# One-lane steps: V's rows and layer B's transposes in another order, layer B on one lane's columns in three more passes, its last pass without mask products

## The chip, the cores and the metric

The kernel runs on one core of one Trainium2 chip. The metric is the device time of one execution in microseconds (us).

## What is computed

Two kinds of layers follow each other four times, A, B, A, B, over 2048 positions of width 640, each with a layernorm ahead of it and a residual sum behind it. A is attention by segments of 32 positions with 32 heads of 192 and 8 memory rows that one segment hands to the next, so its segments must be computed in order. B is attention with 32 heads of 20 over 8 positions of the past, two apart.

```python
# A, for each of the 64 segments s
h = concat([mem, xs])                               # 8 + 32 rows
q, k, v = h @ Wq, h @ Wk, h @ Wv                    # 32 heads of 192
o = softmax(mask(q k^T / sqrt(192))) v @ Wo
mem = o[:8]; outs.append(o[8:])
# B
idx = pos[:, None] - 2 * arange(8)[None, :]         # those below 0 are masked
o = softmax(q . k[idx] / sqrt(20)) v[idx] @ wo
# the whole
x = x + A(layernorm(x)); x = x + B(layernorm(x))
x = x + A(layernorm(x)); x = x + B(layernorm(x))
```

## The kernel before

**Steps and lanes.** The outer loop has 67 steps, t = 0 to 66. Both A layers share their weights, so a step computes one segment of the first A layer (lane 0, segment t) and one of the second (lane 1, segment t - 2) with the same weight loads; a lane has 40 columns (8 memory, 32 new), both have 80. Steps 0 and 1 have lane 0 alone, steps 64 and 65 lane 1 alone (`set_lanes`, `one_lane`). Layer B works one step behind, on `b = t - 1`, also with two lanes of 32 columns: lane 0 is the first B layer, lane 1 the second. Before, B computes all 64 columns in every step from 1 to 65, also in its passes of steps 1, 2 and 65, where only one lane has a segment. The last pass, step 66, is `b_alone`: one lane, nothing of A beside it.

**A step.** Its loop goes over 8 quads of 4 heads: key projection (`a_k`, L264, PSUM bank 0), query projection (bank 1), value projection (bank 2) with transposes in the next quad (`a_vt`), scores, exponential, mask, value product (`a_pv`), normalisation, and the output projection five quads later (`a_o`, L381). In one-lane steps, `a_v_rows` (L298, L299) computes V's rows directly for all quads but 2 and 3: the weights are the moving operand, in two halves of five matmuls of 384 columns, each copied by DVE into `Vt`. The first half uses bank 0 (bank 3 in quad 1), the second bank 2.

**Layer B inside a step.** Its pieces are spread by hand over the quads (`b_first`, `b_second` and `step`): layernorm statistics into bank 3 at quad 0, their centring and scaling by DVE at quad 1 (`ln_center` L456 writes into that bank, `ln_scale` L462 reads it and writes `h2T`), Q and K projections (`b_proj` L495, banks 0 and 3) at quad 1, V at quad 2, the queries spread over heads by POOL (`b_qexp` L526), the scores of four groups of 8 heads (`b_s` L538, banks 0 and 3) with the exponential on ACT and the mask product on DVE (`b_mask` L548), V's transposes (`b_vt` L516, copied by DVE, L520) at quad 3, value products (`b_pv` L561) and norms at quads 5 and 6, transposes of the result at quad 6 (`b_ot` L583) and the output projection (`b_wo` L594). In `b_alone` the same pieces follow each other, with `b_vt`'s two copies on ACT.

**Order.** The kernel writes out the order of PE, ACT, DVE, POOL and SP by hand: each engine takes its instructions in the order of the calls. Of the 64 halves of A's weights 41 stay on the chip; the other 23 are loaded again in each step into a ring of 4 buffers of 480 KB, by two loads of 240 KB each on SP's queue (L226). A ring load is issued when an earlier half's last matmul is done. The input of a step and the output of two segments go over ACT's queue (L606, L609).

Of the kernel before, what the change touches and what calls it, by code (L numbers as in the profile page):

```python
# [10 lines left out]
BF16 = mybir.dt.bfloat16  # L11
F32 = mybir.dt.float32
ACT = mybir.ActivationFunctionType
ALU = mybir.AluOpType
# [3 lines left out]
P = 128  # L18
D = 640
NC = 5  # L20
DH = 192
# [3 lines left out]
SEG = 32  # L25
LT = NM + SEG
NT = 2 * LT
NX = 2 * SEG
LAG = 2
# [4 lines left out]
BD = 20  # L34
BG = 8
# [43 lines left out]
class Kernel:  # L79
# [210 lines left out]
    def a_v_rows(self, i, t):  # L290

        nc = self.nc
        w = [self.units["v", i, h] for h in range(2)]
        vt = self.Vt[0:NT, :].rearrange("p (a b c) -> p a b c", a=2, b=2)
        for h in (1, 0):
            ps = self.big("ps_vr", (3 if i == 1 else 0) if h else 2)
            for c in range(NC):
                nc.tensor.matmul(ps[:, 0:2 * DH], lhsT=self.hT[:, NT * c:NT * c + P], rhs=w[h][:, c, :], start=(c == 0), stop=(c == NC - 1))  # L298
            nc.vector.tensor_copy(out=vt[:, h, :, 0:DH], in_=ps[0:NT, 0:2 * DH].rearrange("p (b c) -> p b c", b=2))  # L299
        self.used("v", i)  # L300

    def a_v(self, i, t):
# [187 lines left out]
    def b_proj(self, part, name, bank):  # L490
        nc = self.nc
        ps = self.big(name, bank)
        for n in range(NC):
            for c in range(NC):
                nc.tensor.matmul(ps[:, NX * n:NX * (n + 1)], lhsT=self.wqkv[:, part, c, P * n:P * (n + 1)], rhs=self.h2T[:, c, :],  # L495
                                 start=(c == 0), stop=(c == NC - 1))
        return ps[:, 0:NC * NX].rearrange("p (n x) -> p n x", n=NC)

    def b_k(self, b):
        self.nc.scalar.copy(out=self.KB[:, :, 64 * (b % 2):64 * (b % 2) + NX], in_=self.b_proj(1, "ps_bk", 3))  # L500

    def b_q(self, b):
        ps = self.b_proj(0, "ps_bq", 0)
        qb = self.bp.tile([P, 6, NX], BF16, name="QB")
        self.nc.scalar.copy(out=qb[:, 0:NC], in_=ps)  # L505
        self.qb = qb

    def b_v(self, b):

        self.nc.scalar.copy(out=self.VTB[:, :, 64 * (b % 2):64 * (b % 2) + NX], in_=self.b_proj(2, "ps_bv", 3))  # L510

    def b_vt(self, copy=None):
        nc = self.nc
        ps = self.ps_big.tile([P, NC, P], BF16, name="ps_bvt", tag="bank3")
        for n in range(NC):
            nc.tensor.transpose(out=ps[:, n, :], in_=self.VTB[:, n, :], identity=self.ident[:])  # L516
        W = BD + 1
        src = ps[:].rearrange("p n e -> p (n e)").rearrange("p (a h d) -> p a h d", a=2, d=BD)
        for par in range(2):
            (copy or nc.vector.tensor_copy)(out=self.VB[:, :, W * par:W * par + BD], in_=src[:, par])  # L520

    def b_qexp(self, c):
        h0, h1 = B_HEADS[c]
        nh = h1 - h0
        qx = self.ap2.tile([P, BG, NX], BF16, name="QX")
        self.nc.gpsimd.tensor_tensor(out=qx[:, 0:nh, :], in0=self.qb[:, c, :].unsqueeze(1).to_broadcast([P, nh, NX]),  # L526
                          in1=self.hmask[c][:].unsqueeze(2).to_broadcast([P, nh, NX]), op=ALU.mult)
        self.qxs[c] = qx

    def b_s(self, g):  # L530

        nc = self.nc
        ps = self.big("ps_bs", 3 * (g % 2))
        parts = [(c, max(h0, BG * g), min(h1, BG * (g + 1))) for c, (h0, h1) in enumerate(B_HEADS)]
        parts = [p for p in parts if p[1] < p[2]]
        for k, (c, lo, hi) in enumerate(parts):
            h0 = B_HEADS[c][0]
            nc.tensor.matmul(ps[:, NX * (lo - BG * g):NX * (hi - BG * g)], lhsT=self.KB[:, c, :],  # L538
                             rhs=self.qxs[c][:, lo - h0:hi - h0, :].rearrange("p h n -> p (h n)"),
                             start=(k == 0), stop=(k == len(parts) - 1), skip_group_check=True)  # L540
        e = self.ebp.tile([P, BG, NX], BF16, name="EB", tag="EB")
        nc.scalar.activation(out=e[:].rearrange("p h n -> p (h n)"), in_=ps[:], func=ACT.Exp, scale=float(BD) ** -0.5)
        self.ebs[g] = e

    def b_mask(self, b, g):
        e = self.ebs[g]
        mask = self.maskB_first.get(b, self.maskB[b % 2])
        self.nc.vector.tensor_tensor(out=e[:], in0=e[:], in1=mask[:].unsqueeze(1).to_broadcast([P, BG, NX]), op=ALU.mult)  # L548

    def b_pv(self, g):  # L550

# [37 lines left out]
    def b_wo(self, b):  # L589
        nc = self.nc  # L590
        ps = self.big("ps_by", 3)
        for n in range(NC):
            for k, piece in enumerate((0, 2, 4, 3, 5)):
                nc.tensor.matmul(ps[:, NX * n:NX * (n + 1)], lhsT=self.wo[:, k, P * n:P * (n + 1)],  # L594
                                 rhs=self.otb[:, piece, :], start=(k == 0), stop=(k == NC - 1))
# [76 lines left out]
    def b_alone(self, b):  # L672

        nc = self.nc
        on = slice(SEG, NX)
        x1 = self.x1.pop(b)
        x = x1[:, 1]
        sq = self.ap1.tile([P, 6, NT], BF16, name="QT")[:, 0:2, :].rearrange("p a n -> p (a n)").rearrange("p (c n) -> p c n", c=NC)
        nc.vector.tensor_tensor(out=sq, in0=x, in1=x, op=ALU.mult)
        ps = self.big("ps_st", 3)  # L680
        for k, v in enumerate((x, sq)):
            for c in range(NC):
                nc.tensor.matmul(ps[:, SEG * k:SEG * (k + 1)], lhsT=self.ones[:], rhs=v[:, c], start=(c == 0), stop=(c == NC - 1))
# [26 lines left out]
        mask = self.maskB[b % 2]  # L710

        def qexp(c):
            h0, h1 = B_HEADS[c]
# [8 lines left out]
        for g in range(NG):  # L722
            ps = self.big("ps_bs", g % 2)
            parts = [(c, max(h0, BG * g), min(h1, BG * (g + 1))) for c, (h0, h1) in enumerate(B_HEADS)]
            parts = [q for q in parts if q[1] < q[2]]
            for k, (c, lo, hi) in enumerate(parts):
                h0 = B_HEADS[c][0]
                nc.tensor.matmul(ps[:, SEG * (lo - BG * g):SEG * (hi - BG * g)].rearrange("p (h n) -> p h n", n=SEG), lhsT=self.KB[:, c, :],
                                 rhs=self.qxs[c][:, lo - h0:hi - h0, :],
                                 start=(k == 0), stop=(k == len(parts) - 1), skip_group_check=True)  # L730
# [4 lines left out]
            nc.vector.tensor_tensor(out=e[:, :, on], in0=e[:, :, on], in1=mask[:, on].unsqueeze(1).to_broadcast([P, BG, SEG]), op=ALU.mult)  # L735
# [22 lines left out]
    def step(self, t):  # L758
# [6 lines left out]
        for i in range(NQUAD - 1):  # L765
# [152 lines left out]
```

## Time and profile before

| | us |
|---|---|
| median of three runs | 3139.08 |
| the runs | 3135.38, 3139.08, 3139.39 |
| profiled execution | 3132.08 |
| its span | 3130.3 |

The span is the time from the first to the last instruction of the profiled execution; 1.8 us of its time lie around it. A stretch of a step is cut at the step's first key projection. In timeline rows the columns are start and length in us, engine, line, operation, what is written from what, shapes, count, and in brackets the idle time of the engine ahead of it and what ended it. The end of a matmul in these rows is modelled and overlaps the next one; the rate is read from start to start.

### The profile page before, as it was taken

How to read it: one execution, taken by the hardware profiler on the slowest of the kernel's cores; microseconds unless marked ns; L12 is line 12 of the kernel's file. 1: busy time of each engine (PE TensorE's matmuls, PEld its weight loads, DVE VectorE, ACT ScalarE, POOL GpSimd, SP SyncE). 2: the span in 40 equal slices, each digit the busy share in tenths (PEclk: the TensorE clock that was granted, in tenths of full speed). 3: DMA queues.
4: the chain of work that ended last, by engine and by line, in shares of the span. 5: the costliest groups of instructions: out<-in, count | busy, mean ns of one | idle time of the engine just before them, and what ended most of it. 6: DMA issues, size and time to landing. Idle time of an engine off the chain costs nothing.

```text
span 3130.3 us, 187135 instructions
## 1 busy us (share of the span) xinstructions
PE 3081.5 (98%) x83420; PEld 3031.5 (97%) x83420; DVE 2376.0 (76%) x6019; ACT 1848.1 (59%) x5613; POOL 553.3 (18%) x1012
## 2 busy tenths in 40 slices
PE   6999999999999999999999999999999999999998
PEld 4899999999999999999999999999999999999997
DVE  3677777777777777777777777777777777777776
ACT  2556656656656656656656656655655656655654
POOL 2111111111111111111111111111111111121121
PEclk7999999999999999999999999999999999999999
DMA  9978887878888887887878878878878878878876
GB/s 386 307 247 246 249 245 246 249 245 248 248 245 250 248 246 246 248 247 246 250 245 248 249 244 248 250 245 249 249 242 251 246 242 252 250 243 249 249 249 214
DMA packets 455705, 786.98 MB, mean 251 GB/s; under 512 B 58864, under 2 KB 445680, under 8 KB 454896
## 3 DMA queue, kind: packets, MB, share of 16 engines
q1 hardware_dynamic: 441216, 769.80, 78.5%
q8 instruction: 652, 10.68, 1.4%
q10 hardware_dynamic: 13680, 5.21, 0.7%
q14 instruction: 157, 1.29, 0.1%
HBM read 772.19 MB, written 2.62 MB: 248 GB/s over the span
## 4 chain that ended last, share of the span: by engine, by line
PE 95%; DMA 3%; DVE 1%; ACT 0%; issue 0%; SPq 0%; ACTq 0%; DVEq 0%
PE ps_acc L381 18%; PE ps_k L264 17%; PE ps_q L264 17%; PE ps_v L264 17%; PE ps_vt L318 5%; PE ps_o L351 5%; PE ps_s L330 2%; PE ps_s L331 2%; PE ps_bs L538 2%; PE ps_by L594 2%; PE ps_bk L495 2%; PE ps_bv L495 1%; PE ps_bq L495 1%; DMA w_k<-in_A_Wk_dram 1%; DMA w_ring<-in_A_Wk_dram 1%; PE ps_vr L298 1%
## 5 line engine op out<-in xcount | busy, mean ns | idle before, releaser
L355 ACT ACTIVATE R<-ps_o 64x160 f32<-64x160 f32 (+1 forms) x2112 | 620.2, 294 | 337.6 <-PE ps_o L351 120.6
L264 PEld LDWEIGHTS <-w_ring 128*128 128x128 bf16 x16530 | 679.7, 100 | 22.2 <-DMA w_ring<-in_A_Wk_dram 4.6
L526 POOL TENSOR_TENSOR QX<-QB,hmask 128x448 bf16<-128x448 bf16 (+1 forms) x325 | 310.6, 964 | 1341.4 <-ACT QB L505 1031.9
L264 PE MATMUL ps_q<-hT,w_q 128*128 128x80 bf16 (+1 forms) x12870 | 541.2, 201 | 4.3 <-DMA w_q<-in_A_Wq_dram 4.1
L264 PEld LDWEIGHTS <-w_q 128*128 128x128 bf16 x12870 | 493.7, 100 | 5.6 <-DMA w_q<-in_A_Wq_dram 5.1
L381 PE MATMUL ps_acc<-OT,w_o 128*128 128x80 bf16 (+1 forms) x9900 | 458.8, 201 | 2.8 <-DMA w_o<-in_A_Wo_dram 2.0
L276 ACT CAST KF<-ps_k 128x320 bf16<-128x320 f32 (+1 forms) x528 | 218.5, 414 | 410.7 <-PE ps_k L264 398.0
L309 DVE CAST vT<-ps_v 128x480 bf16<-128x480 f32 (+1 forms) x504 | 329.0, 653 | 161.7 <-PE ps_v L264 143.5
L283 DVE CAST QT<-ps_q 128x480 bf16<-128x480 f32 (+1 forms) x528 | 337.0, 638 | 118.3 <-PE ps_q L264 114.8
L264 PE MATMUL ps_v<-hT,w_v 128*128 128x80 bf16 (+1 forms) x9480 | 423.3, 201 | 1.3 <-DMA w_v<-in_A_Wv_dram 1.0
L381 PEld LDWEIGHTS <-w_o 128*128 128x128 bf16 x9900 | 393.2, 100 | 3.6 <-DMA w_o<-in_A_Wo_dram 2.3
L264 PE MATMUL ps_k<-hT,w_ring 128*128 128x80 bf16 (+1 forms) x7920 | 375.2, 201 | 6.7 <-DMA w_ring<-in_A_Wk_dram 3.1
L264 PE MATMUL ps_k<-hT,w_k 128*128 128x80 bf16 (+1 forms) x7920 | 374.0, 201 | 2.9 <-issue 1.8
L264 PEld LDWEIGHTS <-w_v 128*128 128x128 bf16 x9480 | 371.4, 100 | 2.1 <-DMA w_v<-in_A_Wv_dram 1.4
L333 ACT ACTIVATE E<-ps_s 80x320 bf16<-80x320 f32 (+1 forms) x528 | 220.7, 418 | 244.6 <-PE ps_s L331 244.6
L365 DVE TENSOR_TENSOR OT<-ps_o,R 128x320 bf16<-128x320 f32 (+1 forms) x528 | 253.8, 481 | 137.5 <-ACT R L357 117.3
L264 PEld LDWEIGHTS <-w_k 128*128 128x128 bf16 x7920 | 321.7, 100 | 3.8 <-issue 2.1
L320 DVE COPY Vt<-ps_vt 80x768 bf16<-80x768 bf16 x504 | 279.2, 554 | 54.1 <-PE ps_vt L318 42.2
L381 PE MATMUL ps_acc<-OT,w_ring 128*128 128x80 bf16 (+1 forms) x5940 | 307.8, 201 | 1.4 <-DMA w_ring<-in_A_Wo_dram 1.3
L264 PE MATMUL ps_v<-hT,w_ring 128*128 128x80 bf16 (+1 forms) x5640 | 264.5, 201 | 0.7 <-DMA w_ring<-in_A_Wv_dram 0.7
L339 DVE TENSOR_TENSOR E<-E,maskA 80x320 bf16<-80x320 bf16 (+1 forms) x528 | 207.4, 393 | 62.2 <-ACT E L333 51.7
L357 ACT ACTIVATE R<-R 128x320 f32<-128x320 f32 (+1 forms) x528 | 244.1, 462 | 16.7
(142 smaller groups left out, 4925.5 us busy)
## 6 DMA issues: line engine op xcount, KB each, us to landing
w_ring<-in_A_Wk_dram SPq DMA_DIRECT2D x1040, 240.0 KB, 3.9
w_ring<-in_A_Wv_dram SPq DMA_DIRECT2D x780, 240.0 KB, 4.0
w_ring<-in_A_Wo_dram SPq DMA_DIRECT2D x780, 240.0 KB, 3.8
w_ring<-in_A_Wq_dram SPq DMA_DIRECT2D x390, 240.0 KB, 4.0
w_q<-in_A_Wq_dram SPq DMA_DIRECT2D x13, 480.0 KB, 8.9
w_v<-in_A_Wv_dram SPq DMA_DIRECT2D x10, 480.0 KB, 9.6
w_o<-in_A_Wo_dram SPq DMA_DIRECT2D x10, 480.0 KB, 9.6
w_ring<-in_A_Wk_dram SPq DMA_DIRECT2D x8, 480.0 KB, 7.3
```

Of the source, the lines that this page charges most:

```text
L264: nc.tensor.matmul(ps[:, NT * n + self.c0:NT * n + self.c1], lhsT=w[n // 3][:, c, P * (n % 3):P * (n % 3 + 1)], rhs=hT[:, NT * c + self.c0 ...
L276: nc.scalar.copy(out=kf, in_=pv[:, :, 0:3:2, :])
L283: self.nc.vector.tensor_copy(out=self.cols(qt[:]), in_=self.cols(ps[:, 0:6 * NT].rearrange("p (a n) -> p a n", a=6)))
L309: nc.vector.tensor_copy(out=self.cols(self.vT[:, 0:6 * NT].rearrange("p (a n) -> p a n", a=6)), in_=self.cols(ps[:, 0:6 * NT].rearrange("p ...
L320: nc.vector.tensor_copy(out=vt[0:NT, :].rearrange("p (a b c) -> p a b c", a=2, b=2)[:, :, :, 0:DH], in_=ps[0:NT].rearrange("p (a b) c -> p ...
L333: nc.scalar.activation(out=self.cols(e[0:NT]), in_=self.cols(sv[0:NT]), func=ACT.Exp, scale=float(DH) ** -0.5)
L339: nc.vector.tensor_tensor(out=self.cols(e[0:NT]), in0=self.cols(e[0:NT]), in1=self.cols(self.maskA[0:NT, :]).unsqueeze(1).to_broadcast([NT ...
L355: nc.scalar.activation(out=self.cols(r[r0:r0 + 64, :, j]), in_=self.cols(src), func=ACT.Ln)
L357: nc.scalar.activation(out=rf, in_=rf, func=ACT.Exp, scale=-1.0)
L365: nc.vector.tensor_tensor(out=oc[:, :, 0:3:2], in0=ov[:, :, 0:4:3], in1=r, op=ALU.mult)
L381: nc.tensor.matmul(self.cols(acc[:, k]), lhsT=w[m // 3][:, m % 3, P * c:P * (c + 1)], rhs=self.cols(ot[:, m]), start=(i == 0 and m == 0 an ...
L526: self.nc.gpsimd.tensor_tensor(out=qx[:, 0:nh, :], in0=self.qb[:, c, :].unsqueeze(1).to_broadcast([P, nh, NX]), in1=self.hmask[c][:].unsqu ...
```

## The change

1. `a_v_rows`: at quad 1 the first half uses bank 2 and the second bank 3. At quad 0 ACT copies the first half instead of DVE.
2. `self.on` holds the columns of B's lanes of the step. Projections, `b_qexp`, scores, exponentials, masks and the output projection work on these columns; `b_vt`, `b_pv`, `b_norm` and `b_ot` keep their size. In the steps with one B lane (1, 2, 65), POOL sets the idle lane's part of each `EB` tile to 1.
3. In one-lane steps `b_vt` is called ahead of the scores of quad 3, and `b_ot` after the value product of quad 6.
4. `b_alone`: POOL makes `low` from the mask, 0 where allowed and -30000 where not; each group's scores begin with a product of the identity with `low`, and the mask products on DVE go. One of `b_vt`'s two copies moves from ACT to DVE.

```diff
+        b = t - 1
+        self.on = slice(SEG * int(b >= self.n_seg), SEG * (1 + int(b >= LAG)))
...
-            ps = self.big("ps_vr", (3 if i == 1 else 0) if h else 2)
+            ps = self.big("ps_vr", ((2, 3) if i == 1 else (0, 2))[1 - h])
...
-            nc.vector.tensor_copy(out=vt[:, h, :, 0:DH], in_=ps[0:NT, 0:2 * DH].rearrange("p (b c) -> p b c", b=2))
+            (nc.scalar.copy if i == 0 and h else nc.vector.tensor_copy)(out=vt[:, h, :, 0:DH], in_=ps[0:NT, 0:2 * DH].rearrange("p (b c) -> p b c", b=2))
...
-                nc.tensor.matmul(ps[:, NX * n:NX * (n + 1)], lhsT=self.wqkv[:, part, c, P * n:P * (n + 1)], rhs=self.h2T[:, c, :],
+                nc.tensor.matmul(ps[:, NX * n + self.on.start:NX * n + self.on.stop], lhsT=self.wqkv[:, part, c, P * n:P * (n + 1)], rhs=self.h2T[:, c, self.on],
...
-            (copy or nc.vector.tensor_copy)(out=self.VB[:, :, W * par:W * par + BD], in_=src[:, par])
+            (copy if copy and par == 0 else nc.vector.tensor_copy)(out=self.VB[:, :, W * par:W * par + BD], in_=src[:, par])
...
-        self.nc.gpsimd.tensor_tensor(out=qx[:, 0:nh, :], in0=self.qb[:, c, :].unsqueeze(1).to_broadcast([P, nh, NX]),
+        self.nc.gpsimd.tensor_tensor(out=qx[:, 0:nh, self.on], in0=self.qb[:, c, self.on].unsqueeze(1).to_broadcast([P, nh, n]),
...
+        whole = self.on.stop - self.on.start == NX
+        flat = (lambda v: v.rearrange("p h n -> p (h n)")) if whole else (lambda v: v[:, :, self.on])
...
+        if not whole:
+            nc.gpsimd.memset(e[:, :, SEG - self.on.start:NX - self.on.start], 1.0)
-        nc.scalar.activation(out=e[:].rearrange("p h n -> p (h n)"), in_=ps[:], func=ACT.Exp, scale=float(BD) ** -0.5)
+        nc.scalar.activation(out=flat(e[:]), in_=flat(sv), func=ACT.Exp, scale=float(BD) ** -0.5)
...
-        if i == 6:
+        if i == 6 and not self.one_lane():
             self.b_ot()
+        if i == 3 and self.one_lane():
+            self.b_vt()
         if 2 <= i <= 3:
             self.b_s(2 * i - 4)
-        if i == 3:
+        if i == 3 and not self.one_lane():
             self.b_vt()
...
+        low = self.bp.tile([P, SEG], BF16, name="low")
+        nc.gpsimd.tensor_scalar(out=low[:], in0=self.maskB[b % 2][:, on], scalar1=1.0, scalar2=30000.0, op0=ALU.subtract, op1=ALU.mult)
         self.warm(36)
...
+            nc.tensor.matmul(ps[:, 0:BG * SEG].rearrange("p (h n) -> p h n", n=SEG), lhsT=self.ident[:],
+                             rhs=low[:].unsqueeze(1).to_broadcast([P, BG, SEG]), start=True, stop=False, skip_group_check=True)
...
-            nc.vector.tensor_tensor(out=e[:, :, on], in0=e[:, :, on], in1=mask[:, on].unsqueeze(1).to_broadcast([P, BG, SEG]), op=ALU.mult)
...
             if i >= 1:
                 self.a_pv()
+            if b is not None and i == 6 and self.one_lane():
+                self.b_ot()
             self.a_v(i, t)
```

`b_k`, `b_q`, `b_v`, `b_mask` and `b_wo` are narrowed to `self.on` in the same way.

More of the change, by code (lines that the diff above doesn't have):

```diff
@@ L494, in b_proj, with b_cols @@
             for c in range(NC):
-                nc.tensor.matmul(ps[:, NX * n:NX * (n + 1)], lhsT=self.wqkv[:, part, c, P * n:P * (n + 1)], rhs=self.h2T[:, c, :],
+                nc.tensor.matmul(ps[:, NX * n + self.on.start:NX * n + self.on.stop], lhsT=self.wqkv[:, part, c, P * n:P * (n + 1)], rhs=self.h2T[:, c, self.on],
                                  start=(c == 0), stop=(c == NC - 1))
-        return ps[:, 0:NC * NX].rearrange("p (n x) -> p n x", n=NC)
+        return ps[:, 0:NC * NX].rearrange("p (n x) -> p n x", n=NC)[:, :, self.on]
+    def b_cols(self, t_, b):
+        o = NX * (b % 2)
+        return t_[:, :, o + self.on.start:o + self.on.stop]
     def b_k(self, b):
-        self.nc.scalar.copy(out=self.KB[:, :, 64 * (b % 2):64 * (b % 2) + NX], in_=self.b_proj(1, "ps_bk", 3))
+        self.nc.scalar.copy(out=self.b_cols(self.KB, b), in_=self.b_proj(1, "ps_bk", 3))
     def b_q(self, b):
@@ L504, in b_q @@
         qb = self.bp.tile([P, 6, NX], BF16, name="QB")
-        self.nc.scalar.copy(out=qb[:, 0:NC], in_=ps)
+        self.nc.scalar.copy(out=qb[:, 0:NC, self.on], in_=ps)
         self.qb = qb
     def b_v(self, b):
-        self.nc.scalar.copy(out=self.VTB[:, :, 64 * (b % 2):64 * (b % 2) + NX], in_=self.b_proj(2, "ps_bv", 3))
+        self.nc.scalar.copy(out=self.b_cols(self.VTB, b), in_=self.b_proj(2, "ps_bv", 3))
     def b_vt(self, copy=None):
@@ L547, in b_mask @@
         mask = self.maskB_first.get(b, self.maskB[b % 2])
-        self.nc.vector.tensor_tensor(out=e[:], in0=e[:], in1=mask[:].unsqueeze(1).to_broadcast([P, BG, NX]), op=ALU.mult)
+        n = self.on.stop - self.on.start
+        self.nc.vector.tensor_tensor(out=e[:, :, self.on], in0=e[:, :, self.on], in1=mask[:, self.on].unsqueeze(1).to_broadcast([P, BG, n]), op=ALU.mult)
     def b_pv(self, g):
@@ L709, in b_alone @@
         nc.scalar.copy(out=self.KB[:, :, k0:k0 + SEG], in_=proj(1, "ps_bk", 3))
-        mask = self.maskB[b % 2]
         def qexp(c):
```

14 lines of the change are left out of this document (8 added, 6 removed).

## The prediction

> **What bounds the kernel now.** I read the page first, then busy time by stretches cut at the steps (a step is one t of the outer loop, 0 to 66), then the list of waits of each stretch that the change touches, then the timeline at the few places that it edits.
>
> ```profile
> span 3130.3 us, 187135 instructions
> ...
> PE 95%; DMA 3%; DVE 1%; ACT 0%; issue 0%; SPq 0%; ACTq 0%; DVEq 0%
> ...
> w_ring<-in_A_Wk_dram SPq DMA_DIRECT2D x1040, 240.0 KB, 3.9
> ```
>
> PE carries 95% of the chain that ended last. The profiled execution took 3132.08 us, 1.8 more than its span; the three plain runs lie at 3135.38, 3139.08 and 3139.39. I sum against 3132.08 and carry the difference to the median, 3139.08. In these four executions nothing under about 0.2% (6.3 us) can be told from no change.
>
> The stretches, in order: step 0, 1, 2, 3 (a full one), 64, 65, and the last pass alone:
>
> ```profile
> 0.00:84.80 84.80, 52.88 (x1034) 40.60 (x1035) 28.64 (x89) 19.86 (x77) 21.23 (x108) 0.76 1.00 387
> 84.80:129.70 44.90, 40.78 (x1115) 35.02 (x1115) 28.56 (x91) 22.07 (x85) 8.53 (x15) 1.00 0.96 330
> 129.70:177.30 47.60, 46.98 (x1280) 46.55 (x1277) 36.11 (x90) 28.47 (x85) 8.21 (x14) 1.00 0.81 249
> 177.30:224.00 46.70, 46.70 (x1276) 46.42 (x1274) 36.39 (x91) 28.36 (x85) 8.22 (x14) 1.00 0.79 245
> 3032.50:3074.40 41.90, 39.81 (x1122) 34.76 (x1119) 28.78 (x91) 22.06 (x85) 8.66 (x15) 1.00 0.84 268
> 3074.40:3115.10 40.70, 39.44 (x1115) 34.54 (x1114) 26.94 (x84) 21.68 (x83) 5.13 (x6) 1.00 0.79 257
> 3115.10:3130.30 15.20, 7.71 (x178) 6.24 (x177) 6.69 (x23) 4.02 (x13) 0.00 (x0) 0.78 0.03 8
> ```
>
> The columns are length, busy time of PE, weight load, DVE, ACT, POOL, then granted clock, DMA share, GB/s. Step 3 stands for the 61 full steps, 3 to 63: PE is busy for all of its 46.70 us. The order of instructions shows the same shapes there before and after, so 61 x 46.7 us do not move. Step 0 is bound by loading: DMA share 1.00. What can move lies in steps 1, 2, 64, 65 and the last pass. PE's waits in them, in us in total, times, longest; one list each for steps 1, 2, 64, 65 and the last pass:
>
> ```profile
> PE ps_k L264 <- issue: 1.2, 2, 0.8
> PE ps_k L264 <- DMA w_ring<-in_A_Wk_dram: 1.1, 3, 0.4
> PE ps_vr L298 <- DVE h2T L462: 0.6, 1, 0.6
> ...
> ```
>
> ```profile
> PE ps_k L264 <- issue: 0.6, 1, 0.6
> ```
>
> ```profile
> PE ps_k L264 <- DMA w_ring<-in_A_Wk_dram: 0.6, 1, 0.6
> PE ps_vr L298 <- DVE h2T L462: 0.6, 1, 0.6
> PE ps_acc L381 <- issue: 0.4, 1, 0.4
> PE ps_k L264 <- DVE Vt L299: 0.2, 1, 0.2
> ```
>
> ```profile
> PE ps_k L264 <- issue: 0.7, 2, 0.5
> PE ps_vr L298 <- DVE h2T L462: 0.4, 1, 0.4
> ```
>
> ```profile
> PE ps_bt L747 <- DVE On L576: 1.0, 1, 1.0
> PE ps_bo L561 <- DVE On L576: 0.9, 1, 0.9
> PE ps_bo L561 <- ACT VB L520: 0.7, 1, 0.7
> ...
> ```
>
> **V's rows (steps 0, 1, 64, 65).** At quad 1 the first half's product was put in bank 3, which still holds the centred layernorm until DVE has scaled it into h2T: that is the 0.6, 0.6 and 0.4 us. In bank 2 it starts at once, and its 0.8 us cover the scaling; the second half then finds bank 3 free. What is late next is layer B's key projection, which needs bank 3 copied out:
>
> ```profile
> 3040.71 0.89 PE L495 MATMUL ps_bq<-h2T,wqkv_sb 128*128 128x64 bf16 x25
> ...
> 3041.44 0.89 PE L495 MATMUL ps_bk<-h2T,wqkv_sb 128*128 128x64 bf16 x25
> ```
>
> ```profile
> 3040.91 0.55 DVE L299 CAST Vt<-ps_vr 80x384 bf16<-80x384 f32 x1 [0.26 <-PE ps_vr L298]
> ```
>
> This copy ended at 3041.46, 0.75 us after the second half's last matmul was issued (there bq starts, 3040.71); bq covers 0.73 of that, with half the columns 0.63 (below). So bk waits about 0.02 us in step 64 and 0.12 in 65, and with it all that PE has queued behind, the quad's scores first. At quad 0 the first copy goes to ACT, which stands idle there:
>
> ```profile
> 3036.19 0.30 ACT L333 ACTIVATE E<-ps_s 80x160 bf16<-80x160 f32 x1 [2.07 <-PE ps_s L331]
> ```
>
> A copy of about 0.55 us fits in 2.07, ahead of this exponential, and step 64's 0.2 us for Vt goes; without that cover it would cost its 0.55. Gains: step 64 0.8, step 65 0.4 - 0.1 = 0.3; step 1's is taken up below.
>
> **Layer B on one lane's columns (steps 1, 2, 65).** Step 65 against the last pass, which has 32 columns already:
>
> ```profile
> 3082.06 0.89 PE L495 MATMUL ps_bq<-h2T,wqkv_sb 128*128 128x64 bf16 x25
> 3082.79 0.89 PE L495 MATMUL ps_bk<-h2T,wqkv_sb 128*128 128x64 bf16 x25
> ```
>
> ```profile
> 3085.95 0.41 PE L538 MATMUL ps_bs<-QX,KB 128*128 128x448 bf16 x2
> ```
>
> ```profile
> 3117.67 0.78 PE L702 MATMUL ps_bq<-h2T,wqkv_sb 128*128 128x32 bf16 x25 [0.41 <-DVE h2T L696]
> 3118.30 0.78 PE L702 MATMUL ps_bk<-h2T,wqkv_sb 128*128 128x32 bf16 x25
> ...
> 3121.11 0.29 PE L728 MATMUL ps_bs<-QX,KB 128*128 128x128 bf16 x2
> ```
>
> From start to start, 25 matmuls take 0.73 us at 64 columns and 0.63 at 32: 0.10 for each of Q, K, V and output projection, 0.40. A pair of score matmuls takes 0.41 against 0.29: 0.12 x 4 = 0.48. Sum 0.9 us of PE per pass, nothing like half. POOL's products, ACT's exponentials and DVE's masks shrink too, off the path. Added are twelve POOL memsets of 256 elements a row; the nearest row is
>
> ```profile
> masks.py:197 POOL MEMSET ident<- 128x128 bf16 x1 | 0.2, 204 | 0.3 <-POOLq L899 0.3
> ```
>
> 0.2 us for half the size; I take 0.3, bounds 0.2 and 0.4. Each waits for the old readers of its buffer, and POOL's next products (five per pass) are queued behind it, but those lose about half of their work; POOL is busy 8 of 47 us. ACT's exponentials wait for no memset, only the later value products do. I cost it at nothing; exposed, 12 x 0.3 = 3.6 us.
>
> The Trainium skill speaks against this edit: its page "TensorE: Matmul & The Clock Gate", section "Back-to-back issue gap", tables one cost, about 60 cycles, for every width from 1 to 64, so the projections would gain nothing. The trace disagrees: 29 ns each at 64 columns, 25 at 32. By that table the sum would be rival E's.
>
> **Where these gains end up.** Step 2 has DMA share 0.81 and one wait early on, none after: 0.9 stands. Step 1 has DMA share 0.96, and its three ring waits come after quad 1: what PE gains before them it waits out. Left is the output projection behind them, 0.1 (bounds 0 and 0.9 + 0.6). In steps 64 and 65 a ring buffer's load lands some 3.9 us (median) after its issue and may be issued only when an earlier half is done, so gains mostly pull the loads with them, but the last few us of gains before a wait are lost. Step 64 (one ring wait, 0.6): 0.8, bounds 0.2 and 1.4. Step 65 has 0.3 + 0.9 = 1.2 in all, about 0.3 of it just ahead of its issue waits: 0.9, bounds 0.3 and 1.9.
>
> **B's transposes and b_ot (steps 1, 64, 65).** The transposes go ahead of the scores of the same quad, b_ot behind the value products. The waits show neither above 0.1 us; I cost both at nothing, bounds 0 and a gain of 0.1 each. Ahead of their copies on DVE nothing new is queued; what b_ot delays is the output projection, a whole projection later. No DMA changes its order on SP's queue.
>
> **The last pass.** Both VB copies ran on ACT; one goes to DVE, whose own rows for it take 323 ns:
>
> ```profile
> 3121.31 0.76 ACT L520 COPY VB<-ps_bvt 128x320 bf16<-128x320 bf16 x2 [0.26 <-PE ps_bvt L516]
> ```
>
> ```profile
> 3122.83 0.66 DVE L576 TENSOR_TENSOR On<-ps_bo,rB 64x160 bf16<-64x160 f32 x2
> 3123.52 0.29 DVE L735 TENSOR_TENSOR EB<-EB,mB 128x256 bf16<-128x256 bf16 x1
> ```
>
> ```profile
> L520 DVE COPY VB<-ps_bvt x130: 318/323/342, 103.3 to 3091.0; 128x320 bf16<-128x320 bf16 x130
> ```
>
> ```profile
> 3122.12 0.36 PE L561 MATMUL ps_bo<-VB,EB 128*128 128x41 bf16 x8 [0.73 <-ACT VB L520]
> ...
> 3123.55 0.65 PE L561 MATMUL ps_bo<-VB,EB 128*128 128x41 bf16 x8 [0.94 <-DVE On L576]
> ```
>
> The first value product starts 0.4 us earlier, and so On. The second value product waits for On and then, 0.65 long against 0.36 of the first one, for the fourth mask, queued on DVE behind On: another 0.3. Sum 0.7. The four added identity products of 256 columns cost between 0 and the 0.29 us of a score pair of 256 columns each; I take 0.15. They stand ahead of the scores, and PE's 0.7 of waiting before the first value product covers them. If that cover is gone, two lie on the path: 0.3 lost. Bounds 0.3 and 1.0.
>
> **The sum.** 0.1 + 0.9 + 0.8 + 0.9 + 0.7 = 3.4 us: 3132.08 - 3.4 = 3128.7, and from the median 3139.08 - 3.4 = 3135.7.
>
> **Rivals.** B, absorbed: DMA and issue waits in steps 64 and 65 grow by what is gained there. For it: step 64's ring wait, step 65's issue waits. Against it: DMA shares of 0.84 and 0.79. Left 0.9 + 0.7 = 1.6: 3137.5. C, everything counts, and waits go with it: 0.1 + 0.9 + 1.4 + 1.9 + 1.0, step 2's 0.6 and about 0.7 of step 1's: 6.6, to 3132.5, past the bound. For it: issue waits appear where DMA is busiest, so they may be chance of phase. D, slower: issue waits, which the profile puts down to nothing, multiply because PE runs ahead of whatever feeds it in one-lane steps. The lists above have five of them on key projections, up to 0.8 us (step 1). From 3.4 / 0.8, that is five more of the longest, it decides; four more in each of steps 1, 2, 64 and 65 would cost 12.8: 9.4 slower, 3148.5. Against it: step 3, whose weight loads are busy 46.42 of 46.70 us, loses nothing to them. The Trainium skill's page "Runtime: NRT & Kernel Launch", section "Instruction fetch mechanics", says that instructions come in blocks over DMA and that this is mostly hidden; by it D would not happen, and no row here names the cause. E, the 0.10 us between 0.73 and 0.63 belongs to the place, a pass with PE half idle, and not to the width: 0.4 less in steps 2 and 65, 0.1 in step 1, gain 2.5: 3136.6. Against it: bq and bk stand back to back in both rows. This is what the table named above would give.
>
> **How the numbers follow.** Forecast 0.47, B 0.20, C 0.20, D 0.08, E 0.05. The plain runs spread over 4.0 us, so each case gets 2 either way: from C, 3132.5 - 2 = 3130.5; from B, 3137.5 + 2 = 3139.5, and half a us towards D: 3140. Faster by over 0.2% needs 3132.8: over half of C, and a quarter of the forecast by spread and by its bounds, with a little of B: 0.28. Slower: D and a little spread, 0.09. The rest, 0.63, is within 0.2%.
>
> **What would show it.** Right: steps 64 and 65 without a wait of ps_vr for h2T, bk in step 65 with one of about 0.1; projections at 0.63 us in steps 1, 2 and 65; step 2 about 46.7 long, step 1 unchanged near 44.8; the last pass near 14.5; full steps at 46.70. Wrong: issue or ring waits in steps 64 and 65 that grew by over 1 us, POOL releasing PE or ACT, a full step of another length, or a new wait in the last pass for the identity products.

## The result, and the profile after

The changed kernel took 3135.88 us (median of 22 runs) against 3139.86 us of the kernel before (22 runs on the same chip): ratio 0.9987, 95% interval 0.9981 to 0.9992, so 4.0 us faster, 2.5 to 6.0. A second comparison (p_after below) gave 0.9987 again, 0.9976 to 0.9998. The forecast was 3.4 us and 3135.7. One of the 22 runs took 5669.06 us and one of p_cols below 4024.18, at mean granted clocks of 0.82 and 0.71; the ratios leave both out, and without them the two medians are 3135.77 and 3138.28.

The profiled executions say the opposite: that of the changed kernel took 3137.52 us, that of before 3132.08. The first is 1.6 above the median of its kernel, the second 3.3 below the fastest of before's three runs. One profile of each therefore can't be subtracted; it has to be read by steps.

The page of the changed kernel, its span, the queue that carries instructions and the chain that ended last:

```profile
span 3135.8 us, 187153 instructions
...
q8 instruction: 652, 10.68, 1.4%
...
PE 96%; DMA 3%; issue 1%; DVE 0%; ACT 0%; SPq 0%; ACTq 0%
```

Busy time by stretches, the same cut: steps 1, 2, 64, 65 and the last pass (length, then PE, weight load, DVE, ACT, POOL, granted clock, DMA share, GB/s):

```profile
84.44:131.94 47.50, 41.25 (x1118) 35.94 (x1116) 27.52 (x90) 21.29 (x86) 7.52 (x19) 0.93 0.90 307
131.94:178.17 46.23, 46.07 (x1278) 45.94 (x1275) 34.77 (x90) 27.33 (x85) 7.27 (x18) 1.00 0.83 261
3037.99:3080.76 42.77, 39.33 (x1121) 34.60 (x1118) 29.36 (x90) 22.66 (x86) 8.44 (x15) 1.00 0.85 273
3080.76:3121.15 40.39, 38.39 (x1116) 33.81 (x1114) 25.77 (x84) 20.74 (x84) 4.45 (x11) 1.00 0.77 246
3121.15:3135.81 14.66, 7.87 (x182) 6.38 (x181) 5.84 (x20) 3.74 (x12) 0.00 (x0) 0.81 0.03 8
```

Step 2 went from 47.60 to 46.23, step 65 from 40.70 to 40.39, the last pass from 15.20 to 14.66; step 64 grew from 41.90 to 42.77, step 1 from 44.90 to 47.50 (at a granted clock of 0.93). What PE waited for in steps 2, 64, 65 and the last pass:

```profile
PE ps_bk L497 <- issue: 0.2, 1, 0.2
...
PE ps_acc L383 <- issue: 2.2, 2, 1.7
PE ps_v L266 <- issue: 0.9, 1, 0.9
PE ps_o L353 <- DVE Vt L322: 0.3, 1, 0.3
...
PE ps_k L266 <- issue: 1.1, 1, 1.1
PE ps_q L266 <- issue: 0.8, 2, 0.6
...
PE ps_bt L765 <- DVE On L590: 1.0, 1, 1.0
PE ps_bo L575 <- DVE On L590: 0.8, 1, 0.8
PE ps_bo L575 <- DVE VB L527: 0.7, 1, 0.7
...
```

The waits that edit 1 aims at, ps_vr for h2T and ps_k for Vt, are gone. A wait of ps_o for Vt (0.3 us) is new in step 64. Beside it stand 3.1 us of "issue" in step 64 and 1.9 in step 65, time in which PE waited for no other engine and no weight load. The profile of before had 0.4 and 0.7 there.

In the timeline of step 65, layer B's key projection starts 0.81 us after its query projection, which now takes 0.63: the wait for V's second copy that the prediction put at 0.12 is about 0.18. The next two rows of that list which matter are A's projections of 30 matmuls on 40 columns, 0.76 us from start to start, 25 ns each:

```profile
3087.66 0.78 PE L497 MATMUL ps_bq<-h2T,wqkv_sb 128*128 128x32 bf16 x25
3088.47 0.78 PE L497 MATMUL ps_bk<-h2T,wqkv_sb 128*128 128x32 bf16 x25
...
3089.29 0.91 PE L266 MATMUL ps_k<-hT,w_ring 128*128 128x40 bf16 x30
3090.05 0.91 PE L266 MATMUL ps_q<-hT,w_q 128*128 128x40 bf16 x30
```

In the last pass, ACT's copy of VB, DVE's, and the value products on PE, from three lists of the timeline:

```profile
3127.31 0.44 ACT L527 COPY VB<-ps_bvt 128x320 bf16<-128x320 bf16 x1 [0.21 <-PE ps_bvt L523]
...
3127.78 0.33 DVE L527 COPY VB<-ps_bvt 128x320 bf16<-128x320 bf16 x1 [0.73 <-ACT VB L527]
...
3128.16 0.36 PE L575 MATMUL ps_bo<-VB,EB 128*128 128x41 bf16 x8 [0.66 <-DVE VB L527]
...
3129.61 0.36 PE L575 MATMUL ps_bo<-VB,EB 128*128 128x41 bf16 x8 [0.84 <-DVE On L590]
```

The copies were to run side by side, 0.4 us saved. They write the same tile, and DVE, whose wait ended with ACT's copy by its row, started 0.03 us after ACT's end: PE's wait for VB went from 0.73 to 0.66 only. The mask's part came: the second value product takes 0.36 instead of 0.65, since no mask product is left behind On.

### The profile page after: what moved, and what is told of

It reads as the page before. It is cut to its first block, busy times and chain, and to the rows that moved or that the text cites. A ratio compares the mean times of both kernels' runs of the same rounds, so it can differ in the third digit from the quotient of the medians.

```text
span 3135.8 us, 187153 instructions
## 1 busy us (share of the span) xinstructions
PE 3079.3 (98%) x83424; PEld 3031.1 (97%) x83424; DVE 2369.9 (76%) x6012; ACT 1849.2 (59%) x5616; POOL 551.5 (18%) x1025
## 4 chain that ended last, share of the span: by engine, by line
PE 96%; DMA 3%; issue 1%; DVE 0%; ACT 0%; SPq 0%; ACTq 0%
PE ps_acc L383 18%; PE ps_k L266 18%; PE ps_q L266 18%; PE ps_v L266 17%; PE ps_vt L320 5%; PE ps_o L353 5%; PE ps_s L332 2%; PE ps_s L333 2%; PE ps_bs L549 2%; PE ps_bk L497 2%; PE ps_by L608 1%; PE ps_bv L497 1%; PE ps_bq L497 1%; DMA w_q<-in_A_Wq_dram 1%; PE ps_vr L300 1%; PE ps_bo L575 1%
## 5 line engine op out<-in xcount | busy, mean ns | idle before, releaser
L534 POOL TENSOR_TENSOR QX<-QB,hmask 128x448 bf16<-128x448 bf16 (+2 forms) x325 | 304.7, 946 | 1346.1 <-ACT QB L512 1028.2
L320 PE MATMUL ps_vt<-ident,vT 128*128 128x128 bf16 x3024 | 253.4, 220 | 0.9 <-DVE On L590 0.9
```

The lines of the kernel that those rows point to most:

```text
L320: nc.tensor.transpose(out=ps[:, n, :], in_=self.vT[:, NT * n:NT * n + P], identity=self.ident[:])
L534: self.nc.gpsimd.tensor_tensor(out=qx[:, 0:nh, self.on], in0=self.qb[:, c, self.on].unsqueeze(1).to_broadcast([P, nh, n]), in1=self.hmask[ ...
```

## The experiments

**Theories.** F, the forecast: the edits' prices add up and stay. W: the issue waits are PE waiting for its own instructions, which come by DMA beside the weights, so that a faster PE gives part of its gain back as issue waits. B, D and E are the prediction's rivals.

### First four: each part alone

p_before is the kernel before, unchanged.

> The kernel before, unchanged, profiled again. The issue waits of PE (waits that the profile puts down to nothing) came to about 4 us in the profiled execution before and about 13 us in the one after, while steps 64 and 65 without them got shorter. Theory W: these waits vary from execution to execution and belong to neither kernel; then this profile's total lies anywhere between 2 and 15 us, and its span follows them. Theory D of the prediction (the change multiplies them): 3 to 5 us again. The time against itself: ratio 1.000, within 0.001.

p_rows has edit 1 alone:

```diff
-            ps = self.big("ps_vr", (3 if i == 1 else 0) if h else 2)
+            ps = self.big("ps_vr", ((2, 3) if i == 1 else (0, 2))[1 - h])
...
-            nc.vector.tensor_copy(out=vt[:, h, :, 0:DH], ...)
+            (nc.scalar.copy if i == 0 and h else nc.vector.tensor_copy)(out=vt[:, h, :, 0:DH], ...)
```

> Only the part on V's rows (bank order at quad 1, the copy on ACT at quad 0). Forecast: no wait of ps_vr for h2T and none of ps_k for Vt in steps 64 and 65, about 0.8 us in step 64 and 0.4 in 65 less of PE time when issue waits are taken off (the bk projection has 64 columns here, so it hides the copy of bank 3); step 1 unchanged. Time: 1.2 us less, ratio 0.9996. Rival B: those waits come back as ring or issue waits in the same step, 0.

p_cols has edit 2 alone, all the places with `self.on`, such as

```diff
-                nc.tensor.matmul(ps[:, NX * n:NX * (n + 1)], ..., rhs=self.h2T[:, c, :],
+                nc.tensor.matmul(ps[:, NX * n + self.on.start:NX * n + self.on.stop], ..., rhs=self.h2T[:, c, self.on],
```

> Only layer B on one lane's columns in steps 1, 2 and 65. Forecast: 0.63 us from bq to bk in steps 2 and 65, score pairs 0.12 shorter, so step 2 and step 65 0.9 us shorter each without issue waits; no wait for POOL. Time: 1.8 us less, ratio 0.9994. Rival E (width does not count in the projections): 0.5 in each, 1.0 less.

p_last has edit 4 alone:

```diff
+        low = self.bp.tile([P, SEG], BF16, name="low")
+        nc.gpsimd.tensor_scalar(out=low[:], in0=self.maskB[b % 2][:, on], ...)
...
-            nc.vector.tensor_tensor(out=e[:, :, on], in0=e[:, :, on], in1=mask[:, on]...)
```

> Only the last pass. The profile after showed DVE's copy of VB starting behind ACT's copy, not beside it, and the first value product as late as before; so the 0.4 us of the forecast for it should be missing and only the 0.3 for the fourth mask be there. Expected from the statistics matmul to the output projection's start: about 0.25 us less than before (forecast: 0.7). Time: ratio 0.9999, not to be told from 1.

Measured against 3138.99 us of before (35 runs):

| | us | ratio | 95% |
|---|---|---|---|
| p_before | 3138.98 | 1.0003 | 0.9994 to 1.0011 |
| p_rows | 3137.24 | 0.9996 | 0.9988 to 1.0005 |
| p_cols | 3138.28 | 0.9997 | 0.9988 to 1.0006 |
| p_last | 3138.85 | 0.9999 | 0.9990 to 1.0007 |

None can be told from no change; the three together make 0.9992. What they give is profiles. In the table each length is cut as above, and the last column is the sum of issue waits over the whole execution (p_after and v_one_copy, described below, are added):

| | edits | step 1 | step 2 | step 64 | step 65 | last | issue |
|---|---|---|---|---|---|---|---|
| before | none | 44.99 | 47.57 | 41.85 | 40.75 | 15.19 | 3.5 |
| p_before | none | 47.02 | 46.71 | 41.86 | 40.93 | 15.18 | 7.6 |
| p_rows | 1 | 48.90* | 48.32* | 43.23 | 40.02 | 15.13 | 8.9 |
| p_cols | 2 | 48.46* | 47.50* | 41.71 | 42.16* | 14.88 | 9.6 |
| p_last | 4 | 48.55 | 48.31* | 41.76 | 42.40 | 14.92 | 11.1 |
| after | all | 47.50* | 46.23 | 42.77 | 40.39 | 14.66 | 12.5 |
| p_after | all | 46.65* | 45.96 | 42.25 | 41.79* | 14.64 | 7.2 |
| v_one_copy | all, 1 more | 47.08* | 46.80 | 41.05 | 39.73 | 14.14 | 7.9 |

The steps with a star had a granted clock of 0.93 to 0.96. Cut finer, in stretches of 3.3 us, step 2 of p_rows begins with one at 0.53. PE's row just ahead of it, the end of step 1, stands first:

```profile
132.33 0.43 PE L381 MATMUL ps_acc<-OT,w_o 128*128 128x40 bf16 x11 [1.63 <-issue]
...
132.60:135.90 3.30, 3.30 (x59) 3.30 (x56) 2.00 (x6) 0.90 (x3) 0.00 (x0) 0.53 0.51 153
135.90:139.20 3.30, 3.30 (x88) 3.30 (x86) 2.51 (x8) 0.63 (x2) 0.00 (x0) 0.96 0.68 216
139.20:142.50 3.30, 3.30 (x102) 3.30 (x99) 2.73 (x6) 2.85 (x10) 0.00 (x0) 1.00 0.70 224
```

59 matmuls instead of about 100: that step is 48.32 against 46.71 in p_before, 1.6 us, with no wait in its own list. But PE had just waited 1.63 us for "issue". The 14 profiles here together show the same: between step 0 and the last pass their clock records have 65 stretches at half clock, 63 of them 3.4 us long and two 6.8, and ahead of each PE had been idle for 0.9 to 2.6 us out of 3.4, in issue waits, ring waits or others. A long wait can therefore cost about 1.7 us more than its length. Not each one does: x_one_rows below has 1.62 us of idle time in such a stretch and no half clock behind it. Steps with a star are left out below, and with them a part of what waits cost.

Issue waits differ by 9 us between executions, before's own by 4. Step 64 is the clearest: with edit 1 its four profiles have 43.23, 42.77, 42.25 and 41.05 us, mean 42.33; without, 41.85, 41.86, 41.71 and 41.76, mean 41.80. The mean grew by 0.5 us, though the waits for h2T (0.6) and Vt (0.2) went. The four with edit 1 lie 2.2 us apart and one is shorter than all the others, so a loss isn't shown; what is missing is the gain. The step's waits in p_before and in p_rows:

```profile
PE ps_acc L381 <- issue: 0.8, 1, 0.8
PE ps_vr L298 <- DVE h2T L462: 0.6, 1, 0.6
PE ps_v L264 <- issue: 0.4, 1, 0.4
PE ps_k L264 <- DVE Vt L299: 0.2, 1, 0.2
```

```profile
PE ps_acc L381 <- issue: 1.9, 2, 1.4
PE ps_k L264 <- DMA w_ring<-in_A_Wk_dram: 0.9, 1, 0.9
PE ps_v L264 <- issue: 0.5, 1, 0.5
```

The same places, ps_acc and ps_v, wait in both, longer in p_rows. Mean issue wait of step 64: 2.4 us with edit 1, 0.7 without. Less these, the step is 1.1 us shorter; 1.7 are given back. In the three kernels that have edit 3 as well, 0.3 to 0.4 us of ps_o waiting for Vt come on top.

### Four more: the edits, in 65 steps instead of three or four

x_cols does edit 2 in every step and leaves out layer B's second lane. The lines that differ from the changed kernel, whose edits 1, 3 and 4 are taken back too:

```diff
-        b = t - 1
-        self.on = slice(SEG * int(b >= self.n_seg), SEG * (1 + int(b >= LAG)))
+        self.on = slice(0, SEG)
...
-            nc.vector.tensor_tensor(out=self.YT[:, :, o:o + SEG], in0=pv[:, :, SEG:NX], in1=x1[:, 1], op=ALU.add)
+            nc.vector.tensor_tensor(out=self.YT[:, :, o:o + SEG], in0=pv[:, :, 0:SEG], in1=x1[:, 1], op=ALU.add)
```

> The kernel before with edit 2 spread over the whole run: layer B works on lane 0's 32 columns in every step from 1 to 65, and the second B layer's columns are left out (both lanes take lane 0's result). A keeps both lanes. That makes about 64 more narrow passes than the change itself has, in steps where PE is busy throughout. Forecast's price: 0.10 us for each of four projections and 0.12 us for each of four score pairs, 0.88 us a pass: 65 x 0.88 = 57 us faster than before, about 3082 us, and full steps of 45.8 us instead of 46.7. Rival E (the projections gain nothing from the smaller width): 0.48 us a pass, 31 us, about 3108 us. If the twelve POOL memsets of the three passes were exposed at 0.3 us each, four a pass would take back 1.2 us a pass, and this kernel would be 20 us or more slower than before. Absorbed by loads: nothing, 3139 us.

x_one runs the one-lane code in every step and leaves out layer A's second lane:

```diff
-        self.l0, self.l1 = int(t >= self.n_seg), 1 + int(t >= LAG)
+        self.l0, self.l1 = 0, 1
```

> The base for the next two: the kernel before with lane 0 alone in every step from 0 to 65, so that A's second lane is left out and each step runs the one-lane code that the change edits; B keeps 64 columns. Steps 64 and 65 of before took 41.9 and 40.7 us, so 65 steps at about 41.3 us, 72 us for step 0 and 15 us for the last pass: about 2775 us. Each step has before's wait of 0.4 to 0.6 us for h2T at quad 1 (all theories). Theory W (issue waits come from blocks of instructions that are fetched beside the weight loads, and their number differs from one execution to the next): some 0.5 us a step of issue waits, up to 65 of them. Rival D in its own form (they come only at the run's two ends) would show hardly any in the middle.

x_one_rows adds p_rows' edit to it,

> x_one with edit 1 (V's rows: other banks at quad 1, ACT copies the first half of quad 0), in about 65 one-lane steps instead of four. Forecast: 0.4 to 0.8 us a step, as costed for steps 65 and 64: 26 to 52 us faster than x_one, and no wait for h2T. Rival B (loads and issue waits grow by what is gained): at most 0.2 us a step, under 13 us. Rival D (PE running ahead brings more waits than it saves): slower than x_one.

and x_one_both x_cols' edit as well.

> x_one with edits 1 and 2: V's rows, and B on 32 columns in every step (B's second lane is left out too). Forecast: 0.4 to 0.8 us a step for the rows less 0.1 us for layer B's key projection, which then waits for V's copy, and 0.88 us a step for the columns: 1.2 to 1.6 us a step, 77 to 103 us faster than x_one. Rival B: the columns count only where no load is late, under 0.9 us a step in all, less than 58 us. Rival E: 0.4 us a step less than the forecast, 51 to 77 us. Rival D: little gain or none, with issue waits that grow by 1 us a step.

Measured against 3137.05 us of before (7 runs):

| | us | ratio | 95% |
|---|---|---|---|
| x_cols | 3096.70 | 0.9869 | 0.9851 to 0.9888 |
| x_one | 2836.92 | 0.9047 | 0.9017 to 0.9077 |
| x_one_rows | 2817.00 | 0.8983 | 0.8952 to 0.9014 |
| x_one_both | 2814.57 | 0.8978 | 0.8958 to 0.8997 |

The base x_one took 62 us more than the 2775 expected of it: its issue waits are 82 us over the run, where 0.5 us a step had been expected.

**In full steps the columns count.** x_cols is 41 us faster (35 to 47), 0.63 us for each of 65 passes: less than the forecast's 0.88, more than rival E's 0.48. Steps 3 to 63 as one stretch, in before and in x_cols:

```profile
177.31:3032.54 2855.23, 2853.88 (x77597) 2833.84 (x77594) 2220.32 (x5551) 1729.88 (x5185) 501.51 (x854) 1.00 0.80 247
```

```profile
177.50:2994.79 2817.29, 2808.03 (x77596) 2799.90 (x77593) 2138.05 (x5551) 1666.92 (x5185) 443.85 (x1098) 1.00 0.80 251
```

The longest issue wait in that stretch of x_cols:

```profile
PE ps_k L265 <- issue: 2.8, 5, 0.9
```

37.9 us shorter, with issue waits of 7.1 us in place of 0.3: 0.73 a step without them, 0.11 given back. The price itself was right: from start to start, without the waits, the three projections, the score pairs and the output projection take 0.89 us a step less, each projection 0.10 and each pair 0.12. Of that 0.11 came back as issue waits and 0.09 in A's query projections (ps_q). The 244 memsets more on POOL (x1098 against x854) release no wait of PE here.

**In one-lane steps they count for nothing.** The same 61 steps of x_one, x_one_rows and x_one_both:

```profile
172.20:2729.93 2557.73, 2420.65 (x68078) 2116.83 (x68076) 1752.22 (x5551) 1348.45 (x5185) 526.93 (x915) 1.00 0.85 275
```

```profile
174.60:2714.28 2539.68, 2415.36 (x68078) 2116.62 (x68076) 1769.35 (x5490) 1379.17 (x5246) 520.05 (x915) 1.00 0.86 277
```

```profile
173.76:2714.47 2540.71, 2375.53 (x68079) 2084.59 (x68077) 1690.68 (x5490) 1308.40 (x5246) 461.57 (x1159) 0.99 0.86 277
```

The longest of PE's waits in these stretches, in the same order:

```profile
PE ps_vr L298 <- DVE h2T L462: 29.0, 52, 0.6
PE ps_q L264 <- issue: 28.9, 40, 1.8
PE ps_k L264 <- issue: 19.2, 33, 1.6
```

```profile
PE ps_q L264 <- issue: 32.8, 36, 1.9
PE ps_k L264 <- issue: 20.7, 28, 1.6
```

```profile
PE ps_q L265 <- issue: 47.4, 52, 2.1
PE ps_k L265 <- issue: 29.0, 41, 1.6
```

| steps 3 to 63 | length | issue waits | less issue waits |
|---|---|---|---|
| x_one | 2557.7 | 77.5 | 2480.2 |
| x_one_rows | 2539.7 | 91.0 | 2448.7 |
| x_one_both | 2540.7 | 129.0 | 2411.7 |

Edit 1 takes 0.52 us a step out of PE's work and other waits, and 0.22 come back as issue waits; edit 2 takes 0.61, and 0.62 come back. The last column still holds what the half-clock stretches cost; these steps have 5 of them in x_one, 6 in x_one_rows and 12 in x_one_both. By the plain runs x_one_rows is 20 us faster than x_one (0.31 a step, where 0.4 to 0.8 were forecast), x_one_both 22 (0.34). The forecast for x_one_both was 77 to 103, and it lies below rival B's 58 as well. Rival D's mechanism is there, at a price that eats the gain and no more.

### What an issue wait is

The records of DMA transfers in the trace tell more. The queue q8 of the page moved 652 packets of 16,384 bytes in before, and its page counts 83,420 matmuls and as many weight loads: 256 of these for each packet. In x_one_both it is 577 packets and 73,748 of each, 256 again. Counted through the trace (0.18% added for instructions that it does not show), all 177 issue waits of x_one_both stand within two instructions of a multiple of 256; each of those over 0.2 us ends 1.1 to 1.7 us after a q8 packet has landed, one packet for each block of 256. So PE waits there for a block of its own instructions, whose packet was started only after PE had begun the block ahead of it. Times from PE's beginning of one block, medians:

| | packet of the next block starts | has landed | shortest time of a block (1st percentile) |
|---|---|---|---|
| before | 1.2 | 2.3 | 4.3 |
| x_one | 1.9 | 3.0 | 3.3 |
| x_one_both | 1.9 | 3.0 | 3.3 |

With about 1.4 us more from landing to use, a full step, whose matmuls take 46.70 us / 1276 = 37 ns and a block of 128 matmuls and their weight loads 4.7 us, has time to spare: 2.3 + 1.4 is less than 4.7. A row of 40-column projections, 25 ns a matmul and 3.2 us a block, has not: 3.0 + 1.4 is more than 3.2.

### The last four

x_one_thin keeps x_one_both's instructions and takes 40% of the bytes off the ring loads:

```diff
+THIN = 1152
...
-                t_ = self.wring.tile([P, HALF], BF16, name="w_ring")
+                t_ = self.wring.tile([P, THIN], BF16, name="w_ring")
...
-            self.units[key] = t_[:].rearrange("p (a b) -> p a b", a=3 if kind == "o" else NC)
+            if key in self.resident:
+                self.units[key] = t_[:].rearrange("p (a b) -> p a b", a=3 if kind == "o" else NC)
+            else:
+                v = t_[:]
+                self.units[key] = bass.AP(tensor=v.tensor, offset=v.offset, ap=[list(v.ap[0])] + ([[256, 3], [1, 640]] if kind == "o" else [[192, NC], [1, 384]]))
```

> The instructions of x_one_both, with ring loads of 60% of the bytes: a ring buffer holds 1152 of its 1920 elements a row, and the matmuls read them in overlapping pieces (so the streamed weights are not the real ones). Same number of instructions and of loads. x_one_both lost 135 us in 177 issue waits, x_one 82 in 136. Theory W (PE's instructions come in blocks of 256 by DMA, a block is fetched when the one before it is begun, and its fetch queues behind weight packets, so the waits come from PE's speed and DMA's load together): with a DMA share of about 0.55 instead of 0.87 the fetches start at once, the issue waits fall below 45 us and the time by 90 us or more, to about 2715 us; ring waits go too. If the waits come from PE's speed alone (a fixed time from one block to the next): issue waits stay between 110 and 140 us or more, and the time between 2780 and 2815 us.

It took 2618.91 us, ratio 0.8343 (0.8328 to 0.8357): 196 us below x_one_both, at the same number of instructions, and about twice the fall that theory W had expected (to 2715). Steps 3 to 63, and then the waits of that stretch:

```profile
157.81:2532.25 2374.44, 2338.87 (x68078) 2066.16 (x68076) 1681.03 (x5490) 1304.87 (x5246) 465.94 (x1159) 1.00 0.63 181
```

```profile
PE ps_q L274 <- issue: 5.1, 14, 0.8
PE ps_o L361 <- DVE Vt L330: 4.8, 27, 0.4
...
PE ps_k L274 <- issue: 3.6, 8, 0.9
```

Over the whole run the issue waits fell from 135 us in 177 to 14 in 40, DMA share in the steps from 0.86 to 0.63; a packet of instructions starts 1.0 us into the block ahead of it, not 1.9. Theory W holds, and PE's speed alone is ruled out. Of the 189 us between the spans 121 are issue waits and 7 step 0. PE's busy time is 41 us less too (2593 to 2553): the 12 half-clock stretches of steps 3 to 63 are gone, 20 us by an estimate of 1.7 each. The rest is spread over ring waits and pieces that no list shows.

x_one_all is x_one_both with edits 3 and 4; of edit 3:

```diff
+        if i == 3 and self.one_lane():
+            self.b_vt()
...
+            if b is not None and i == 6 and self.one_lane():
+                self.b_ot()
```

> x_one_both with edits 3 and 4: B's transposes ahead of the scores and the transposes of its result behind the value product in 65 one-lane steps, and the last pass's edits (0.5 us once). The prediction cost edit 3 at nothing, bounds 0 and a gain of 0.1 us for each of the two: 0 to 13 us faster than x_one_both, taken: 0. Theory W: what PE gains is given back as issue waits for the most part, so nothing that can be told (x_one_both: 2814.6 us; 2808 to 2820).

2818.54 us, ratio 0.8985 (0.8963 to 0.9008): the same as x_one_both within the intervals. Edit 3 is worth nothing that can be told, in 65 steps. (The profiled execution took 2835.32 us; it has 157 us of issue waits and 24 half-clock stretches in steps 3 to 63.)

p_after is the changed kernel again.

> The changed kernel as it is, a second sample beside new runs of before. Forecast: 3.4 us faster. By the amplified steps (x_cols, x_one, x_one_rows, x_one_both against each other): 0.63 us for step 2, 0.31 to 0.34 for each of steps 1, 64 and 65, and 0.5 for the last pass: 2.1 us faster, a ratio of 0.9993. The first comparison gave 4.0 us (2.5 to 6.0).

3136.22 us against 3139.36 of before (21 runs), ratio 0.9987 (0.9976 to 0.9998). Its profiled execution took 3134.9 us, like p_before's (3134.93). Step 64 in it:

```profile
PE ps_acc L383 <- issue: 1.6, 2, 0.9
PE ps_v L266 <- issue: 1.0, 1, 1.0
PE ps_o L353 <- DVE Vt L322: 0.4, 1, 0.4
```

v_one_copy adds an edit to the changed kernel: both halves of VB in one DVE instruction in the last pass.

```diff
+        if copy:
+            dst = bass.AP(tensor=self.VB.tensor, offset=self.VB.offset, ap=[list(self.VB.ap[0]), [W, 2], [2 * BD + 1, BH // 2], [1, BD]])
+            nc.vector.tensor_copy(out=dst, in_=src)
+            return
         for par in range(2):
-            (copy if copy and par == 0 else nc.vector.tensor_copy)(out=self.VB[:, :, W * par:W * par + BD], in_=src[:, par])
+            nc.vector.tensor_copy(out=self.VB[:, :, W * par:W * par + BD], in_=src[:, par])
```

> The changed kernel with one edit more: in the last pass both halves of VB are copied by one DVE instruction, since ACT's and DVE's copies ran one after the other in the changed kernel (0.44 and 0.33 us, the second one waiting for the first). One instruction of twice the size takes about 0.55 us on DVE: the first value product starts 0.2 us earlier, its wait falls from 0.66 to about 0.45 us, and the last pass ends at about 14.45 us instead of 14.66. In the whole time that can't be told from the changed kernel: within 0.1% of it.

3132.81 us, ratio 0.9977 (0.9968 to 0.9986). DVE's copy and the first value product:

```profile
3124.98 0.51 DVE L528 COPY VB<-ps_bvt 128x640 bf16<-128x640 bf16 x1 [0.26 <-PE ps_bvt L523]
...
3125.54 0.36 PE L579 MATMUL ps_bo<-VB,EB 128*128 128x41 bf16 x8 [0.36 <-DVE VB L528]
```

The wait fell from 0.66 to 0.36 (expected 0.45), the last pass from 14.66 and 14.64 to 14.14 us. It has the lowest time of all kernels here that do the whole work, and is faster than before beyond its interval. That it is 3.4 us faster than the changed kernel by the medians can't be upheld: the profile shows 0.5 us for it, and the two intervals overlap.

## Why the prediction was right, and where its steps were not

The time came out: 3135.7 forecast, 3135.88 measured. That they lie so close is in part luck. The base under the forecast, 3139.08, came from three runs and is 3139.86 over 22, and the terms of the sum came out unevenly. The account by steps, from the profiles without a star:

- **Step 2, 0.9.** 47.57 and 46.71 before, 46.23, 45.96 and 46.80 after; less their issue waits (0.6, 0, 0.2, 0, 0.7), 46.8 against 46.0: 0.8. Projections went from 0.73 to 0.63 as said. By x_cols the price is right (0.89 us of PE time a full step) and 0.63 to 0.73 of it reach the time. Rival E's 0.48 lies outside x_cols' interval; so does the one cost for widths from 1 to 64 that the Trainium skill tables ("TensorE: Matmul & The Clock Gate", "Back-to-back issue gap").
- **Step 64, 0.8.** Wrong. The waits went, and less issue waits the step is 1.1 shorter, within the bounds of 0.2 and 1.4. Yet the gain isn't there: the mean is 0.5 longer, from four profiles 2.2 us apart. The step that failed is "gains mostly pull the loads with them". For ring loads it can't be told (ring waits of 0.5 to 0.9 stand in two of the four profiles without edit 1 and in one of the four with it); PE's instruction blocks were not thought of, and their waits took back 1.7. A loss in this step was allowed for in rival D alone. That step 3 loses nothing to issue waits was no evidence against D: a full step takes 37 ns a matmul, a one-lane projection 25.
- **Step 65, 0.9.** 40.75, 40.93 and 42.40 without edits 1 and 2, 40.39 and 39.73 with both: 1.3 in the means (issue waits of 0.2 to 1.8 without, 0 and 1.9 with). Without the 42.40 it is 0.8, and with p_after's starred 41.79 it is 0.7. Right in sign; the size can't be told from two and three samples. The wait of bk was there, 0.18 for 0.12.
- **Step 1, 0.1.** 44.99 to 48.55 without the edits: can't be told. The forecast of "near 44.8" took one execution for the rule.
- **The last pass, 0.7.** 0.5 (15.18 to 14.66 and 14.64). Identity products hidden and mask products 0.3, as costed; the failed term is the 0.4 for two copies side by side, which wrote one tile and ran one after the other, so the wait for them fell by 0.07.
- **Edit 3 and the memsets, nothing.** Right in the main: x_one_all gained nothing, x_cols shows no wait for POOL, and x_one_both one of 1.5 us in 65 passes. But a wait of ps_o for Vt, 0.3 to 0.4 us in step 64, stands in the three of the eight profiles that have edit 3 and in no other; why is open.

Added up, 0.8 - 0.5 + 1.3 + 0.5 = 2.1 us, from so few samples that each of the middle two may be off by half a us or more; the amplified runs give 0.63 + 3 x 0.33 + 0.5 = 2.1 too. That is between rival B's 1.6 and the forecast's 3.4, and just below the 2.5 to 6.0 of the first comparison, inside the 0.6 to 7.5 of the second. The direction is shown. Which share of the measured 4.0 is the change, and where 2 us of it would lie, stays open: no step shows them, and 0.1% is as little as these runs tell apart. The 61 full steps, whose instructions the change leaves alone, took 2855.2 us in before and 2857.2 to 2861.7 in the other seven profiles, so the prediction's "full steps at 46.70" was one execution too, and these steps alone vary by more than the change is worth.

Rival B's mechanism (issue waits grow by what is gained) holds in step 64 and, by x_one_both, for edit 2 in one-lane steps. Rival D's is the same mechanism at a price of 0.2 to 0.6 us a step, where D needed 3.2. In "Runtime: NRT & Kernel Launch", "Instruction fetch mechanics", the Trainium skill says that crossing a block boundary is mostly hidden. The traces agree for full steps (0.3 to 5.0 us in 61 of them, in the eight profiles of the table) and not for one-lane steps (77.5 to 152 us in 61).

## What to carry to other kernels

A gain on an engine's own time is worth what its supplies allow: when matmuls get shorter beside heavy loads, count how long a block of 256 of PE's instructions takes and look for "issue" waits that are not there yet. A wait of over a us may also bring a stretch at half clock: look at the granted clock behind it, too. Price such an edit in the steps where it will run, not in the busiest steps, and where it occurs three times only, repeat it in all steps of an experiment: 0.3 us can be read from 65 of them, not from one. Two engines that copy into one tile do not run side by side until the trace shows it; one larger instruction was cheaper.

## What was not expected of the hardware

Instruction blocks cost this kernel 3.5 to 12.5 us an execution, in places that change from one execution to the next; in kernels of one-lane steps it is 82 to 157 us, and 14 with 40% less weight traffic. A packet of instructions took about 1.0 us, but started 1.0 to 1.9 us after PE had begun the block ahead of it, later where DMA was busier. And a wait may cost more than its length. Where PE had been idle for 0.9 to 2.6 us out of 3.4, the granted clock was at half for the next 3.4 us in 63 cases and for 6.8 in two, about 1.7 us lost in 3.4 (0.53 over 3.3 us and 59 matmuls in p_rows). In steps 3 to 63 there were none of these in before and x_one_thin, 5 in x_one, 12 in x_one_both and 24 in x_one_all. Issue waits and half-clock stretches may be most of the 4 us by which runs of the same kernel differ; only the profiled executions show them, so this is not shown.
